# A gated-recurrence and SwiGLU kernel on one core: new dates in its planner, another count of its clock fillers, and another way to narrow its weights

## The chip, the cores and the metric

The kernel runs on one core of one Trainium2 chip. The metric is the device time of one execution in microseconds (us). A core has TensorE (PE, with its weight loads as PEld), VectorE (DVE), ScalarE (ACT), GpSimd (POOL) and SyncE (SP), which here only issues DMAs; ACT and POOL issue some too. Each engine runs its own list of instructions in order and waits for semaphores of the others.

## What is computed

Four sequences of 768 steps with 8 heads of 48 features go through a recurrence with a complex gate per feature. Its output, 3072 tokens of 384 features, goes through a root-mean-square norm and a SwiGLU feed-forward:

```python
mag = np.sqrt(a_re * a_re + a_im * a_im)
scale = np.minimum(mag, 0.999) / (mag + 1e-06)
a_re_n, a_im_n = (a_re * scale, a_im * scale)
for t in range(S):
    new_re = ar * S_re - ai * S_im          # ar, ai: the gate at step t
    new_im = ar * S_im + ai * S_re
    S_re, S_im = (new_re + kv, new_im)      # kv: outer product of k and v at t
    y[:, :, t] = np.einsum('bhd,bhde->bhe', q[:, :, t], S_re)
...
xn = x / rms * rms_g                        # x: y as 3072 x 384
g = xn @ w_gate
silu = g * (1.0 / (1.0 + np.exp(-g)))
val = xn @ w_val
return (silu * val @ w_out)
```

The three weights (384 x 1536, 384 x 1536, 1536 x 384) come as 64-bit floats, all else as 32-bit floats.

## The kernel before

**Tiling.** The 3072 tokens are 24 chunks of 128 steps, six to a sequence. Gates are worked out in *units*: chunk 0, chunk 1, and then two chunks at a time (`gates`, line 1138). A unit loads the gate's parts and q and k, takes the gate's size (stage "size"), running products and a root ("root"), the running angle with sine and cosine ("turn"), and rotates q and k ("rot"): the products go to the tiles `rot` or `kin`. Six DMAs per chunk on SP then bring them from there into the tile `kq`, one partition set at a time (line 1229). `attend` (line 1247) multiplies k by q of a chunk on PE (`bank<-kq`), masks the scores into `am` on VectorE, makes the output y and the new state, and norms it into `xT`. Two chunks are a group of the feed-forward. The first two groups run plainly (`feed`), the other ten with products of sums of blocks, in which fewer block products are needed (`joint`, `forms`).

**Weights.** `narrow` (line 1035) turns a 64-bit float into a 32-bit one in 12 pieces: six of 1536 values per partition (gate and value weights by turns) and six of 768 (output weights). POOL fetches the raw words piece by piece (`fetch`, line 1012), two ahead at most; the fifth fetch also waits for `cleared[1]`, a one-column copy `seen<-kq` on POOL that shows that the second chunk's rotated rows have landed. With `lo` and `hi` the two 32-bit words of a value, ScalarE scales `lo` down to the last three bits, and VectorE shifts `hi` left by three, clears two exponent bits and keeps the sign with one scalar_tensor_tensor (`stt`), and adds `lo`. The integer sum shows in the profile as CUSTOM_DVE_ANT_0.

**The order of the work** is not written by hand. The code first hands each operation to a planner, `Flow`, with a duration, what it reads and writes, and sometimes a due date. `dates` (line 595) derives due dates backwards from the feed-forward's clock and adds a shift per stage from `flow.shift` (line 1675). `schedule` (line 617) plays the operations through a model of the engines and the DMA queue: of those that are ready on an engine it takes the one due first, and the result is each engine's fixed order. A DMA is landed, in this model, a time `load` of service plus `slow` plus 1.0 us after its turn. Neither `slow` nor `load` nor any duration is an instruction; they only move the order. `issue` (line 741) emits everything, so that nearly all rows of the profile bear line 746.

**Fillers.** After idle time PE runs matmuls slowly at first (15 filler records start between 26 and 29 us, 29 between 31 and 34). Where PE has a gap ahead of its next operation before 62 us (`WARM`), the planner puts matmuls without use into it (lines 707 to 713), of rows of `rot`, which show as `bank<-rot`. They can only start once the first rotated rows of the first chunk are written (`started`). The count is made from the gap in the model:

```python
since = max([free["PE"]] + [x["end"] + 0.06 for x in self.warm["after"] if not recent])
step = 0.26 if recent else 0.43
n = int((t - since - 0.25) / step)
```

`recent` holds the last PE operations of any kind, `free["PE"]` is the end of PE's last one, `t` the start of the next.

**Closing check.** At the end of its work the kernel also looks at all raw weights again (`look`, line 1056) and at ranges of the gates; a slower general version runs where a limit is passed, which the inputs here don't.

Of the kernel before, what the change touches and what calls it, by code (L numbers as in the profile page):

```python
# [8 lines left out]
FP32 = mybir.dt.float32  # L9
I32 = mybir.dt.int32  # L10
U32 = mybir.dt.uint32
I16 = mybir.dt.int16
BF16 = mybir.dt.bfloat16
AF = mybir.ActivationFunctionType
ALU = mybir.AluOpType
PSUM = bass.MemoryType.PSUM
# [2 lines left out]
P = 128  # L19
# [481 lines left out]
class Flow:  # L501
# [10 lines left out]
    turn = 0.0  # L512
# [104 lines left out]
    def schedule(self):  # L617
# [3 lines left out]
        free = {}  # L621
# [10 lines left out]
        recent = []  # L632
# [13 lines left out]
        while True:  # L646
# [58 lines left out]
                dur += self.between(o, last)  # L705
                mode, last = o["mode"], o
            if eng == "PE" and self.warm and not claimed and t < self.warm["until"] and all("end" in x for x in self.warm["after"]):
                since = max([free["PE"]] + [x["end"] + 0.06 for x in self.warm["after"] if not recent])
                step = 0.26 if recent else 0.43
                n = int((t - since - 0.25) / step)  # L710
                if n > 0:
                    self.fillers.append((order - 0.5, n))
                    recent.append((since, since + step * n))
            claimed = claimed or o["claims"]
            if eng == "PE":
                busy = sum(min(e, t) - max(b, t - 4.0) for b, e in recent if e > t - 4.0)
# [32 lines left out]
def fast(tc, ctx, qT, kT, v, a_re, a_im, w_gate, w_val, w_out, rms_g, out, H, bad):  # L749

    nc = tc.nc
# [28 lines left out]
    def room(name, shape, dtype=FP32):  # L780
        t = mem.tile(shape, dtype, name=name, tag=name)
        row = 1
        for x in shape[1:]:
            row *= x
        rooms[t.tensor.name] = (name, row * mybir.dt.size(dtype))
        keep.append(t)
        return t
# [122 lines left out]
    width = room("width", [P, 1])  # L910
    warm = room("warm", [P, 1])
    gcol = room("gcol", [P, ND])
    zeros = room("zeros", [P, 2 * C])
    ends = room("ends", [P, ND, N])
    range_ = room("range_", [P, NU])
# [66 lines left out]
    for r in range(ND):  # L982
        o = pick[:, r].rearrange("p (x j) -> p x j", j=2 * ND)[:, :, r::ND]
        copy(o, band.unsqueeze(2).to_broadcast([P, P // H, 2]), late=LATE)
    dma(gcol, rms_g.rearrange("(c p) -> p c", p=P))

# [23 lines left out]
    def fetch(i, piece, raw, eng):  # L1012
        to, ap, c, f = piece
        rows, n = to.shape[1:]
        src = ap.bitcast(I32).rearrange("(c p) f -> p c f", p=P)[:, c, 2 * f:2 * (f + n)]
        raw3 = raw.rearrange("p (c f) -> p c f", c=rows)
        if eng == "POOL" and i >= AHEAD:
            wait = [landed[i - AHEAD]]
        elif eng == "POOL":
            wait = [begun[0]]  # L1020
        else:
            wait = []
        if eng == "POOL" and i in CLEAR:
            wait = wait + [cleared[CLEAR[i]]]
        pace = dict(load=1.9 + 1.0e-3 * raw.shape[1], lead=1.2) if eng == "POOL" else dict(slow=2.5)
        sent = dma(raw3, src, eng, after=wait, **pace)
        if eng == "POOL":
            landed[i] = add("POOL", [(nc.gpsimd.tensor_copy, (), dict(out=junk, in_=raw[0:1, 1:2]))], 0.4,
                            after=[sent])
        words = raw.rearrange("p (n two) -> p n two", two=2)  # L1030
        return words[:, :, 0], words[:, :, 1]

    HALVED = ()

    def narrow(i):
        flow.stage = "w", i
        to, ap, c, f = pieces[i]
        rows, n = to.shape[1:]
        if ap.dtype == FP32:
            dma(to, ap.rearrange("(c p) f -> p c f", p=P)[:, c, f:f + n], "POOL")  # L1040
            return
        flow.stage = "raw", i
        lo, hi = (x.rearrange("p (c f) -> p c f", f=n) for x in fetch(i, pieces[i], places[i], "POOL"))
        flow.stage = "w", i
        t = to.bitcast(I32)
        act(lo, lo.bitcast(U32), AF.Copy, scale=2.0 ** -29)
        step = n // 2 if i in HALVED else n
        for f in range(0, n, step):
            to_, lo_, hi_ = (x[:, :, f:f + step] for x in (t, lo, hi))
            add("DVE", [(nc.vector.tensor_scalar, (),  # L1050
                         dict(out=to_, in0=hi_, scalar1=3, scalar2=None, op0=ALU.logical_shift_left))],
                0.15 + 0.52e-3 * rows * step, [hi_], [to_])
            stt(to_, hi_, 0x3FFFFFFF, to_, ALU.bitwise_or, ALU.bitwise_and)
            tt(to_, to_, lo_, ALU.add)

    def look(i):
        flow.stage = "look", i
# [80 lines left out]
    def gates(u):  # L1138
# [85 lines left out]
        for i, n_ in enumerate(ns):  # L1224
            if i and n_ >= SOLO:
                yield "moves"
            kq = kqs[n_ % 2 if n_ < SOLO else 0]
            flow.stage = "rot", u
            moved[n_] = [dma(kq[r:D2:2 * ND], x, "SP", slow=0.3) for r, x in enumerate(rows[n_])]
            if n_ < 2:  # L1230
                cleared[n_] = copy(seen, kqs[n_ % 2][0:D2, 0, 0:1], eng="POOL")
                cleared[n_]["dur"] = 0.25
            if not i:
                send_decays(u)
# [12 lines left out]
    def attend(n):  # L1247
# [74 lines left out]
        act(sq, yT, AF.Square)  # L1322
        if unit_of[n] in LIGHT:
            for j in range(ND):
                act(yg[:, j], yT[:, j], AF.Copy, scale=gcol[:, j:j + 1])
        else:
            tt(sq[:, 0], sq[:, 0], sq[:, 1], ALU.add)
            tt(sq[:, 0], sq[:, 0], sq[:, 2], ALU.add)
# [52 lines left out]
    def feed(g, xT):  # L1381
# [41 lines left out]
        for i in range(2):  # L1423
            o = bank()[:, 0:DM]
            for f0 in range(0, NF, 4):
                clock[0] += 4 * mm_time(DM) * SPREAD
                mms([(o, h[:, i, f], wo[:, f], f == 0, f == NF - 1) for f in range(f0, f0 + 4)],
                    4 * mm_time(DM), due=clock[0])
            act(ots[i], o, AF.Copy)
        finish(ns)  # L1430

    def finish(ns):
# [186 lines left out]
    for n in range(N):  # L1619
        for x in rest:  # L1620
            pass
        while gated < NU and UNITS[gated][0] <= n:
            rest = gates(gated)
            for x in rest:
                if x:
                    break
            gated += 1
        xT = attend(n)
        g = group_of[n]
        if n == GROUPS[g][-1] and g < WIDE:  # L1630
            if g < PLAIN:
                feed(g, xT)
            else:
                joint(g, sets, range(5))
            if g == FIRST - 1:
                flow.stage = "feed", FIRST
                weight_sums()
                flow.stage = "scale", 0
                for f in range(DF // W):
                    for w_ in (wg, wv):  # L1640
                        for d in range(ND):
                            act(w_[:, f, d], w_[:, f, d], AF.Copy, scale=gcol[:, d:d + 1])
            if g == PLAIN - 1:
                sets = forms()

# [11 lines left out]
    for in_, limit, op in ((ef, P_MIN, ALU.is_ge), (ef, 1.0, ALU.is_le), (range_, 0.0, ALU.is_le),  # L1657
# [15 lines left out]
    flow.warm = dict(after=started, until=WARM, call=[  # L1673
        (nc.tensor.matmul, (banks[3][:, 0:C],), dict(lhsT=filler[:, 0:C], rhs=filler[:, C:2 * C], start=True, stop=True))])
    flow.shift = {
        ("attend", 6): -2.0, ("attend", 10): 27.7, ("attend", 13): -59.0, ("attend", 15): -9.6,
        ("attend", 16): 3.2, ("attend", 18): -0.6, ("attend", 19): 3.8, ("attend", 20): -8.6,
        ("attend", 21): 8.9, ("decay", 2): 9.4, ("feed", 0): 12.3, ("feed", 1): 8.8, ("feed", 2): 0.1,
        ("feed", 3): 33.4, ("feed", 4): 12.1, ("feed", 5): 22.8, ("feed", 6): 10.8, ("feed", 7): 19.1,
        ("feed", 8): -3.7, ("feed", 9): -0.3, ("feed", 11): -8.6, ("form", 3): 18.9, ("form", 5): -0.3,  # L1680
        ("form", 11): -0.7, ("head", 1): 0.4, ("head", 2): -5.2, ("kq", 3): -1.8, ("load", 0): 0.2,
        ("load", 1): -0.9, ("look", 3): 1.0, ("look", 4): -3.5, ("look", 6): 2.0, ("look", 11): 17.2,
        ("look", 13): 50.4, ("look", 17): 28.6, ("norm", 2): -0.7, ("norm", 8): 9.0, ("norm", 9): -8.6,
        ("norm", 12): 1.9, ("norm", 22): -30.7, ("norm", 23): -5.1, ("raw", 0): -5.9, ("raw", 1): 2.7,
        ("root", 2): 4.2, ("root", 5): 0.1, ("root", 9): 0.2, ("root", 10): 0.2, ("root", 11): 0.1,
        ("root", 12): 0.2, ("rot", 1): 91.2, ("rot", 6): 43.0, ("rot", 8): -1.0, ("size", 0): 0.5,
        ("size", 1): -2.6, ("size", 3): 59.1, ("size", 8): 0.9, ("size", 9): -4.8, ("size", 10): 32.3,
        ("size", 11): 3.3, ("size", 12): 29.3, ("state", 1): -32.4, ("state", 3): -12.7, ("state", 6): -11.7,
        ("state", 7): 1.5, ("state", 14): -0.6, ("state", 18): -9.4, ("state", 19): -9.8, ("state", 20): -11.4,
        ("state", 21): -1.1, ("state", 22): 0.4, ("turn", 3): -0.4, ("turn", 5): -0.1, ("turn", 6): 66.3,  # L1690
        ("turn", 7): 41.7, ("turn", 8): 1.9, ("w", 1): 25.0, ("w", 2): -1.5, ("w", 3): -4.7, ("w", 4): 18.1,
        ("w", 5): 37.1, ("w", 10): 9.8, ("y", 3): 0.9, ("y", 6): -2.3, ("y", 12): 17.5, ("y", 14): 3.9,
        ("y", 18): 2.4, ("y", 23): -6.5,
    }
    flow.schedule()
    with tc.manual_schedule():
# [56 lines left out]
```

## Time and profile before

| what | us |
|---|---|
| median of 3 runs | 691.67 |
| lowest to highest run | 690.75 to 694.41 |
| the profiled execution | 691.83 |
| its span in the profile | 690.1 |
| granted TensorE clock, mean | 0.996 |

A row of a timeline has start and length in us, engine, line, operation, output and inputs with shapes, how many it merges, and in brackets the idle time before it with what ended it. A row of the groups has busy us and mean ns behind the first bar, idle time and its releasers behind the second. A row of the stretches has its length, then busy time and number of instructions by engine, the granted clock, the share of the DMA engines and GB/s. A matmul of 32-bit floats shows as two records.

### The profile page before, as it was taken

Reading aid. Unit: us, or ns where it says so; the run is one execution under the profiler, and the core shown is the slowest. Engines: PE = TensorE matmul, PEld = TensorE weight load, DVE = VectorE, ACT = ScalarE, POOL = GpSimd, SP = SyncE. Lnnn points to the kernel's source line nnn. Section 1 sums busy time; section 2 is a strip of 40 time slices with the busy share of each in tenths; the row PEclk is TensorE's granted clock in tenths of the full one; section 3 lists DMA queues with packets and bytes.
Section 4 is the critical chain, followed back from the end, with each engine's and each line's share of the span. In section 5 each row is a group of like instructions: output and inputs, shape, how many; then the busy total and the mean of one; then the engine's idle time right before and its main releaser. Section 6 shows DMA issues by size and latency. Waiting matters only on the chain.

```text
span 690.1 us, 19118 instructions
## 1 busy us (share of the span) xinstructions
PE 652.9 (95%) x7965; PEld 609.6 (88%) x7965; DVE 556.2 (81%) x1026; ACT 499.6 (72%) x864; POOL 63.7 (9%) x109
## 2 busy tenths in 40 slices
PE   0699999999999999999999999989999998999997
PEld 0688887786899999999999999989999998999997
DVE  8969999989998969879989869779879777346563
ACT  8629667895685774874788776867679675799872
POOL 3113031011000100011010100101000000000000
PEclk9999999999999999999999999999999999999999
DMA  9786574355325521354552622556151445735510
GB/s 282 257 230 195 146 208 140 98 128 107 102 54 97 140 34 54 92 117 79 141 89 61 146 53 45 115 107 143 39 107 34 95 128 116 258 95 184 161 47 26
DMA packets 104156, 81.98 MB, mean 119 GB/s; under 512 B 41953, under 2 KB 94561, under 8 KB 104065
## 3 DMA queue, kind: packets, MB, share of 16 engines
q1 hardware_dynamic: 98560, 64.68, 35.0%
q0 software_dynamic: 4416, 15.35, 10.5%
q8 instruction: 63, 1.03, 0.6%
q10 hardware_dynamic: 1088, 0.69, 0.3%
q14 instruction: 29, 0.23, 0.1%
HBM read 55.84 MB, written 4.72 MB: 88 GB/s over the span
## 4 chain that ended last, share of the span: by engine, by line
PE 76%; DVE 8%; issue 4%; SPq 4%; DMA 4%; ACT 3%; POOL 0%; DVEq 0%; POOLq 0%; ACTq 0%
PE bank L746 76%; SPq L746 4%; DVE turns L746 1%; DVE hT L746 1%; DVE t L746 1%; DMA decay<-ends 1%; ACT in L746 1%; ACT t L746 1%; DMA in<-in_w_val_dram 1%; DMA ve<-in_v_dram 1%; DVE rot L746 1%; DVE am L746 1%; ACT L746 1%; DMA vn<-in_v_dram 1%; ACT bank L746 1%
## 5 line engine op out<-in xcount | busy, mean ns | idle before, releaser
L746 PE MATMUL bank<-wo,hT 128*128 128x192 f32 (+1 forms) x696 | 140.7, 350 | 0.0
L746 PEld LDWEIGHTS bank<-wo,hT 128*128 128x128 f32 x696 | 115.0, 190 | 11.6 <-DVE hT L746 0.5
L746 PE MATMUL bank<-xT,wg 128*128 128x128 f32 (+1 forms) x488 | 85.3, 308 | 0.0
L746 PE MATMUL bank<-xT,wv 128*128 128x128 f32 (+1 forms) x488 | 83.2, 303 | 0.0
L746 ACT ACT_TABLE_LOAD x57 | 73.1, 1283 | 9.4 <-DVE rot L746 5.1
L746 ACT ACTIVATE hT<-bank 128x512 f32<-128x512 f32 x100 | 58.4, 596 | 25.0 <-PE bank L746 22.5
L746 PEld LDWEIGHTS bank<-xT,wg 128*128 128x128 f32 x488 | 71.4, 193 | 5.3 <-issue 0.6
L746 PEld LDWEIGHTS bank<-xT,wv 128*128 128x128 f32 x488 | 70.6, 193 | 3.2 <-issue 0.2
L746 POOL TENSOR_TENSOR rs<-ssv,mhalf 128x1 f32<-128x1 f32 x24 | 21.4, 890 | 461.5 <-ACT ssv L746 407.9
L746 DVE COPY_PREDICATED am<-causal,bank 128x512 f32<-128x512 int32 x48 | 34.7, 731 | 22.9 <-PE bank L746 22.8
L746 DVE TENSOR_TENSOR hT<-hT 128x768 f32<-128x768 f32 (+1 forms) x60 | 51.5, 860 | 0.4
L746 PE MATMUL bank<-yg,wg 128*128 128x128 f32 x320 | 50.7, 281 | 0.0
L746 PE MATMUL bank<-yg,wv 128*128 128x128 f32 x320 | 48.8, 275 | 0.0
L746 ACT ACTIVATE bank<-bank 128x512 f32<-128x512 f32 x60 | 35.2, 586 | 17.9 <-PE bank L746 11.4
L746 ACT ACTIVATE sg<-bank 128x256 f32<-128x256 f32 (+1 forms) x72 | 38.5, 536 | 9.2 <-DVE bank L746 4.7
L746 DVE TENSOR_TENSOR hT<-bank,hT 128x512 f32<-128x512 f32 x50 | 34.3, 687 | 13.4 <-ACT bank L746 5.3
L746 PE MATMUL bank<-sums,hT 128*128 128x192 f32 x240 | 44.7, 329 | 0.0
L746 PEld LDWEIGHTS bank<-yg,wg 128*128 128x128 f32 x320 | 42.2, 191 | 1.3 <-issue 0.2
L746 PEld LDWEIGHTS bank<-yg,wv 128*128 128x128 f32 x320 | 42.2, 192 | 0.0
L746 PEld LDWEIGHTS bank<-kq 96*32 96x32 f32 x1536 | 30.5, 110 | 11.2 <-issue 5.1
L746 PEld LDWEIGHTS bank<-sums,hT 128*128 128x128 f32 x240 | 39.1, 190 | 0.4 <-DVE mid L746 0.2
L746 PE MATMUL bank<-kq 96*32 96x128 f32 (+3 forms) x1536 | 36.4, 237 | 3.1 <-DMA decay<-ends 1.9
(217 smaller groups left out, 1451.5 us busy)
## 6 DMA issues: line engine op xcount, KB each, us to landing
kq<-rot SPq DMA_DIRECT2D x84, 128.0 KB, 2.5
kq<-kin SPq DMA_DIRECT2D x60, 128.0 KB, 2.6
kin<-in_q_dram SPq DMA_DIRECT2D x24, 192.0 KB, 2.9
kin<-in_k_dram SPq DMA_DIRECT2D x24, 192.0 KB, 3.3
in<-in_a_re_dram SPq DMA_DIRECT2D x11, 384.0 KB, 4.2
in<-in_a_im_dram SPq DMA_DIRECT2D x11, 384.0 KB, 4.2
out_dram<-ot SPq DMA_DIRECT2D x22, 192.0 KB, 3.0
vn<-in_v_dram SPq DMA_DIRECT2D x20, 192.0 KB, 3.2
```

The source lines that it names most:

```text
L746: fn(*args, **kw)
```

## The change

It has four parts.

1. *Fillers.* The end of what the fillers read now always counts, and the number depends on whether PE was busy for 2 of the last 4 us before the gap; the first nine of a cold gap are taken as slow.

```diff
-                since = max([free["PE"]] + [x["end"] + 0.06 for x in self.warm["after"] if not recent])
-                step = 0.26 if recent else 0.43
-                n = int((t - since - 0.25) / step)
+                since = max([free["PE"]] + [x["end"] + 0.06 for x in self.warm["after"]])
+                left_ = t - since - 0.25
+                hot = sum(e - max(b, since - 4.0) for b, e in recent if e > since - 4.0)
+                n = int(left_ / 0.24 if hot >= 2.0 else left_ / 0.43 if left_ < 3.9 else 9 + (left_ - 3.9) / 0.24)
                 if n > 0:
                     self.fillers.append((order - 0.5, n))
-                    recent.append((since, since + step * n))
+                    recent.append((since, t - 0.25))
```

2. *Narrowing.* ScalarE writes the last bits as a 16-bit number into the lower half of the word `lo` and the sign of `hi` as a 16-bit float (+1 or -1) into its upper half. Adding that word to the shifted `hi` gives sign, exponent and last bits at once, and half the weight's value. The `stt` is gone.

```diff
-        act(lo, lo.bitcast(U32), AF.Copy, scale=2.0 ** -29)
-        step = n // 2 if i in HALVED else n
-        for f in range(0, n, step):
-            to_, lo_, hi_ = (x[:, :, f:f + step] for x in (t, lo, hi))
-            add("DVE", [(nc.vector.tensor_scalar, (),
-                         dict(out=to_, in0=hi_, scalar1=3, scalar2=None, op0=ALU.logical_shift_left))],
-                0.15 + 0.52e-3 * rows * step, [hi_], [to_])
-            stt(to_, hi_, 0x3FFFFFFF, to_, ALU.bitwise_or, ALU.bitwise_and)
-            tt(to_, to_, lo_, ALU.add)
+        low, high = (places[i].bitcast(d).rearrange("p (c f four) -> p c f four", f=n, four=4)[:, :, :, k]
+                     for d, k in ((U16, 0), (BF16, 1)))
+        act(low, lo.bitcast(U32), AF.Copy, scale=2.0 ** -29)
+        act(high, hi.bitcast(FP32), AF.Sign)
+        add("DVE", [(nc.vector.tensor_scalar, (),
+                     dict(out=t, in0=hi, scalar1=3, scalar2=None, op0=ALU.logical_shift_left))],
+            0.15 + 0.52e-3 * rows * n, [hi], [t])
+        tt(t, t, lo, ALU.add)
```

3. *Scales.* The halved weights are made up for by factors of 2: two new columns `gate_col` and `val_col` take the place of `gcol` where weights and the first norms are scaled, and a plain group's output copy gets a scale.

```diff
+    MORE = [1.0 if x.dtype == FP32 else 2.0 for x in (w_gate, w_val, w_out)]
+    act(gate_col, gcol, AF.Copy, scale=MORE[0])
+    act(val_col, gcol, AF.Copy, scale=MORE[1] * MORE[2])
...
-                act(yg[:, j], yT[:, j], AF.Copy, scale=gcol[:, j:j + 1])
+                act(yg[:, j], yT[:, j], AF.Copy, scale=gate_col[:, j:j + 1])
...
-            act(ots[i], o, AF.Copy)
+            act(ots[i], o, AF.Copy, scale=MORE[2])
```

4. *The planner's numbers.* The rotated rows are taken as 1.5 us slower to land from the third chunk on (0.3 before), the first four weight fetches as quicker, and the table of shifts is replaced: 87 entries of -59.0 to 91.2 go, 11 small ones come.

```diff
-        pace = dict(load=1.9 + 1.0e-3 * raw.shape[1], lead=1.2) if eng == "POOL" else dict(slow=2.5)
+        pace = dict(load=1.9 + (0.8e-3 if i < 4 else 1.0e-3) * raw.shape[1], lead=1.2) if eng == "POOL" else dict(slow=2.5)
...
-            moved[n_] = [dma(kq[r:D2:2 * ND], x, "SP", slow=0.3) for r, x in enumerate(rows[n_])]
+            moved[n_] = [dma(kq[r:D2:2 * ND], x, "SP", slow=0.3 if n_ < 2 else 1.5) for r, x in enumerate(rows[n_])]
...
+        ("feed", 1): 5.5, ("feed", 2): 0.1, ("feed", 10): -0.1, ("look", 6): 0.1, ("look", 7): -1.6,
+        ("norm", 22): -0.3, ("root", 3): 0.1, ("rot", 0): 0.5, ("turn", 3): -0.1, ("y", 7): -0.3, ("y", 16): 0.1,
```

More of the change, by code (lines that the diff above doesn't have):

```diff
@@ L13 @@
 BF16 = mybir.dt.bfloat16
+U16 = mybir.dt.uint16
 AF = mybir.ActivationFunctionType
@@ L912, in fast @@
     gcol = room("gcol", [P, ND])
+    gate_col = room("gate_col", [P, ND])
+    val_col = room("val_col", [P, ND])
     zeros = room("zeros", [P, 2 * C])
@@ L1031, in fetch @@
         return words[:, :, 0], words[:, :, 1]
-    HALVED = ()
     def narrow(i):
@@ L1639, in fast @@
                 for f in range(DF // W):
-                    for w_ in (wg, wv):
+                    for w_, col in ((wg, gate_col), (wv, val_col)):
                         for d in range(ND):
-                            act(w_[:, f, d], w_[:, f, d], AF.Copy, scale=gcol[:, d:d + 1])
+                            act(w_[:, f, d], w_[:, f, d], AF.Copy, scale=col[:, d:d + 1])
             if g == PLAIN - 1:
@@ L1675, in fast @@
     flow.shift = {
[L1676 to L1693, printed above, removed]
+        ("feed", 1): 5.5, ("feed", 2): 0.1, ("feed", 10): -0.1, ("look", 6): 0.1, ("look", 7): -1.6,
+        ("norm", 22): -0.3, ("root", 3): 0.1, ("rot", 0): 0.5, ("turn", 3): -0.1, ("y", 7): -0.3, ("y", 16): 0.1,
     }
```

## The prediction

> **What bounds the kernel now.** I read the page's busy shares first.
>
> ```profile
> PE 652.9 (95%) x7965; PEld 609.6 (88%) x7965; DVE 556.2 (81%) x1026; ACT 499.6 (72%) x864; POOL 63.7 (9%) x109
> ```
>
> PE is the bound. Busy time by stage says where it isn't full:
>
> ```profile
> 56.00:120.00 64.00, 62.92 (x651) 53.16 (x651) 61.85 (x87) 48.12 (x68) 12.95 (x16) 1.00 0.57 171
> 120.00:480.00 360.00, 356.24 (x4612) 329.74 (x4611) 313.92 (x594) 263.71 (x441) 29.05 (x44) 1.00 0.43 95
> 480.00:690.00 210.00, 203.61 (x2216) 198.28 (x2215) 136.12 (x275) 153.89 (x297) 6.70 (x12) 0.99 0.39 108
> ```
>
> The columns are PE, PEld, DVE, ACT, POOL. From 56 us on PE is busy 622.8 of 634 us (62.92 + 356.24 + 203.61). So what starts the feed-forward earlier reaches the end nearly one for one. Nearly all idle time of PE lies before 56, and what it is busy with there is not all work. The timeline of PE, then of its neighbours:
>
> ```profile
> 16.95 2.38 PE L746 MATMUL bank<-ot,ot 128*96 128x8 f32 x12 [16.95 <-DVE ot L746]
> 25.70 14.31 PE L746 MATMUL bank<-rot 128*128 128x128 f32 x108 [6.37 <-DVE rot L746]
> 39.94 1.33 PE L746 MATMUL bank<-kq 96*32 96x128 f32 x64
> 45.14 1.33 PE L746 MATMUL bank<-kq 96*32 96x128 f32 x64
> 56.17 2.84 PE L746 MATMUL bank<-xT,wg 128*128 128x128 f32 x24
> ...
> 25.67 3.82 SPq L746 DMA_DIRECT2D kq<-rot  x6
> 31.61 0.49 POOL L746 COPY seen<-kq 96x1 f32<-96x1 f32 x1 [2.92 <-DMA kq<-rot]
> 31.97 1.82 DVE L746 TENSOR_TENSOR rot<-kin,turns 128x768 f32<-128x768 f32 x2
> 32.95 4.78 SPq L746 DMA_DIRECT2D kq<-rot  x6
> 40.80 1.37 DVE L746 COPY_PREDICATED am<-causal,bank 128x512 f32<-128x512 int32 x2 [6.14 <-PE bank L746]
> 41.79 0.89 ACT L746 ACTIVATE kt<-bank 128x384 f32<-128x384 f32 x2 [11.78 <-PE bank L746]
> 47.33 0.80 POOL L746 DMA_DIRECT2D wo<-in_w_gate_dram  x1
> ```
>
> `bank<-rot` is the filler that keeps the clock up: 108 records, two to a matmul, so 54 fillers in 14.31 us. The first chunk's attend (kq, 39.94) stands behind them, though its data had landed by 31.61: **8.3 us of late start made by the fillers themselves**. Others pay too: VectorE is held 6.14 us and ScalarE 11.78 us by that attend, and the fifth weight fetch (47.33), which comes on POOL behind the second `seen`, waits as well.
>
> **The change part by part.**
>
> *Fillers.* Line 708 takes the data's end into account only while no PE work is recent. The decay products (16.95 to 19.33) made it recent, so fillers were counted from about 19.3, while they can start only with rot, 25.70. 54 x 0.26 + 0.25 = 14.3 us from 19.3 puts the planner's start of the attend at about 33.6 at the latest; the real data say 31.6. The new count starts from rot's end: 25.7 + 0.25 to 31.6 or 33.6 leaves 5.65 to 7.65 us, and 9 + (left - 3.9) / 0.24 gives 16 to 24 fillers. What they take, by the records and busy time of the fillers in two stretches:
>
> ```profile
> 26.00:29.00 3.00, 3.00 (x15) 1.00 0.53 149
> 31.00:34.00 3.00, 3.00 (x29) 1.00 0.40 64
> ```
>
> Fifteen filler records in 3 us early, 29 later: 0.40 us and 0.21 us a filler. Nine slow ones and 7 to 15 quick ones take 5.1 to 6.8 us and end at 30.8 to 32.5. With the data at 31.6, the first attend starts at 31.7 to 32.6; I take 32.2, **7.7 us earlier**.
>
> Next is the second chunk. Its six kq transfers are issued from 32.95, over 4.78 us; the first chunk's, issued over 3.82, took from 25.67 to 31.61 from first issue to landing, so the second's are there at 38.9 to 39.9. Its attend therefore can't slide from 45.14 by all of 7.7: in the old order it gains 5.2 to 6.2, middle 5.7, and more if rot of chunk two goes ahead (it ran at 31.97, and its transfers waited in SP's order behind five ve loads). From there to the feed's start the old dates took 56.17 - 45.14 = 11.0 us, with two of the 1.75 us operations of the next part between; I let a little over half of one come through, 1.0: **feed 6.7 us earlier**, with 4.5 (as if the second attend lost 1.2 more) and 9 (7.7 and most of both operations) as bounds. Late next could be the weights of the feed's last third; their fetch (47.33) waits for the second chunk's landing, so it moves up to about 40, as far as the feed does.
>
> *Conversion of the weights.* Per piece a scalar_tensor_tensor on VectorE goes, and a Sign on ScalarE comes:
>
> ```profile
> L746 DVE SCALAR_TENSOR_TENSOR wo<-hT,wo 128x768 int32<-128x768 int32 x4 | 3.8, 954 | 0.0
> L746 DVE SCALAR_TENSOR_TENSOR wv<-wo,wv 128x1536 int32<-128x1536 int32 x2 | 3.5, 1754 | 0.0
> L746 DVE SCALAR_TENSOR_TENSOR wg<-wo,wg 128x1536 int32<-128x1536 int32 x2 | 3.5, 1752 | 0.0
> L746 DVE SCALAR_TENSOR_TENSOR wo<-wo 128x768 int32<-128x768 int32 x2 | 1.9, 952 | 0.0
> L746 DVE SCALAR_TENSOR_TENSOR wv<-hT,wv 128x1536 int32<-128x1536 int32 x1 | 1.8, 1752 | 0.0
> L746 DVE SCALAR_TENSOR_TENSOR wg<-hT,wg 128x1536 int32<-128x1536 int32 x1 | 1.7, 1748 | 0.0
> ...
> L746 ACT ACTIVATE t<-t 128x768 f32<-128x768 f32 x33 | 27.7, 841 | 11.0 <-DVE t L746 10.8
> L746 ACT ACTIVATE wo<-wo 128x1536 int32<-128x1536 uint32 x4 | 6.5, 1633 | 0.0
> ...
> 10.00:120.00 110.00, 93.06 (x1140) 81.62 (x1141) 99.25 (x141) 74.66 (x114) 23.22 (x28) 1.00 0.69 209
> ```
>
> VectorE loses 3.8 + 3.5 + 3.5 + 1.9 + 1.8 + 1.7 = 16.2 us, all within 10 to 120 us, where it is busier than PE (99.25 of 110). The trace has no Sign. By the nearest rows, a 1536-wide one lies between twice 0.84 less one fixed part (about 1.5) and 1.63; a half-size one is about 0.85. I take 1.5: 6 x 1.5 + 6 x 0.85 = 14.1 us on ScalarE, which has 110 - 74.7 = 35.3 us idle there; 7.7 of those go with the fillers, 13.5 remain. That idle hides the Signs; without it up to 14.1 us would show. For the path to the feed's start I count nothing beyond the 1.0 above. Past it, two waits on VectorE may go, 0.62 and 0.46 us; I take **1.0 us**.
>
> *The two new columns.* gate_col and val_col are two tiny ScalarE instructions that wait for gcol:
>
> ```profile
> 8.97 0.59 SPq L746 DMA_DIRECT2D gcol<-in_rms_g_dram  x1
> gcol<-in_rms_g_dram SPq DMA_DIRECT2D x1, 1.5 KB, 10.2
> 85.15 0.55 PE L746 MATMUL bank<-ident,kq 96*128 96x96 f32 x4 [0.62 <-DVE am L746]
> 96.47 0.71 PE L746 MATMUL bank<-ident,kq 96*128 96x96 f32 x6 [0.46 <-DVE xT L746]
> ```
>
> Issued at 8.97, gcol lands near 19.2. Behind a waiting column stand the gates of both first chunks on ScalarE: placed at 17 it would cost them 2 us, placed in the 11.78 us of idle time ahead of 41.79 nothing. The planner picks by due date, and the first reader is the first norm, later than those gates; I take 0. The other scale changes alter a number in an instruction that is there already.
>
> *New dates.* No instruction appears; orders on every engine change. The larger slow for kq from the third chunk on only makes the planner expect what the late transfers show here:
>
> ```profile
> 550.07 0.39 SPq L746 DMA_DIRECT2D in<-in_w_gate_dram  x1
> 562.57 0.39 SPq L746 DMA_DIRECT2D in<-in_w_val_dram  x1
> 572.22 0.99 PE L746 MATMUL bank<-kq 96*32 96x128 f32 x32 [1.93 <-DMA decay<-ends]
> 573.14 1.22 PE L746 MATMUL bank<-xT,wg 128*128 128x128 f32 x4
> 575.86 0.69 PE L746 MATMUL bank<-xT,wv 128*128 128x128 f32 x4
> 464.24 0.52 PE L746 MATMUL bank<-ident,kq 96*128 96x96 f32 x4 [2.14 <-issue]
> ```
>
> SP stood 12 us between two loads of the closing check, the transfers behind the second went out late, and PE waited 1.93 us; then its groups of four matmuls took 1.22 instead of 0.69 until 575.9, some 1.4 us more over three of them. With the 2.14 at 464.24, about 5.5 us after 400 could go. The bounds are those 5.5 gained, and as much lost to new waits of the same kind; I take **2.0 us** gained, nearer to nothing.
>
> **The sum.** 6.7 + 1.0 + 2.0 = 9.7. The profiled execution took 691.83 us (span 690.1), the median is 691.67: 691.83 - 9.7 = 682.1, on the median 682.0.
>
> **The rivals.**
>
> *All of it lands* (0.18): the second attend moves up by the whole 7.7 or more (rot of chunk two goes ahead), VectorE's relief pulls the feed 9 us earlier, and most of the 5.5 go: 691.7 - 9 - 1 - 5 = about 677 down to 673. For it: VectorE's 6.14 us of idle time and 16.2 us of work go in the same stretch. Against: SP's issue, 12 transfers of about 0.6 us and five loads in one queue.
>
> *The head start is spent again* (0.12): the feed starts 4.5 earlier, and the new order makes about 2 to 4 us of waits more than the old one had: 688 to 691. For it: the old order has only about 11 us of PE idle after 56, so there is more to lose than to win. Against: the wait at 572 is on transfers that were expected too early, which the new times correct.
>
> *Slower: Sign isn't in the active table* (0.08). The chip loads an activation table where a function is missing:
>
> ```profile
> L746 ACT ACT_TABLE_LOAD x57 | 73.1, 1283 | 9.4 <-DVE rot L746 5.1 <-issue 2.3 <-DVE kin L746 1.1
> 20.44 1.28 ACT L746 ACT_TABLE_LOAD   x1
> 22.67 1.68 ACT L746 ACTIVATE wo<-wo 128x1536 int32<-128x1536 uint32 x1
> ```
>
> If each of 12 Signs needs its own and the next function loads again, 24 x 1.283 = 30.8 us come to 14.1, 44.9 us on ScalarE where 35.3 - 7.7 = 27.6 are idle. The 17.3 us over delay the rotations and so the attends: 682 + 17.3 = 699, slower than before. It decides from one load per Sign (15.4 + 14.1 = 29.5, just full) upwards. Against it: Copy runs at 22.67 right behind a load for Sin, with none of its own.
>
> The Trainium skill, "ScalarE: Activation LUTs", section "Table sets: the hidden batching unit", says that cheap functions such as relu, copy, identity and abs stand in every set, but Sign is not among those it names there. The Copy row agrees with it; by its wording Sign would be free if it counts as cheap, and the rival's 30.8 us would hold if not. No run here shows a Sign yet.
>
> **How the numbers follow.** Forecast 682.0, chance 0.62, own range 677 to 687. The range 673 to 690 takes in the full landing and most of the spent start, and leaves out the table rival and the tails. About 0.5% is what a measurement of this kernel tells from no change: faster means below 688.2. From forecast 0.62, full landing 0.18 and a third of the spent start 0.04: faster 0.84; same 0.08; slower 0.08.
>
> **What would show it.** Fillers: about 32 to 48 `bank<-rot` records in the first gap and the first kq matmul near 32 us; wrong if it starts after 34, or if VectorE's idle before the first `am` stays above 3 us. Second attend at 38 to 40.5; feed at 47 to 52 instead of 56.17. Conversion: no scalar_tensor_tensor of int32 pieces, 12 new activations at 0.85 and 1.5 us, still 57 table loads or nearly; over 65 would prove the table rival. Dates: PE busy share from the feed's start on at 98% or more; a share below means new waits, and then the time comes out above 687. The forecast is wrong if the feed starts early and PE then starves for the third and fourth chunk or for weights.

## The result and the profile after

| what | us |
|---|---|
| before, median of 4 runs | 691.36 (690.75 to 694.41) |
| after, median of 4 runs | 711.51 (710.88 to 711.96) |
| ratio | 1.0284, 95% interval 1.0256 to 1.0311 |
| predicted | 682.0 (673 to 690) |

The changed kernel is slower by 2.8%. The page's busy shares, which stand in the order of those before:

```profile
PE 659.9 (93%) x7934; PEld 613.3 (86%) x7935; DVE 543.7 (77%) x1014; ACT 551.5 (78%) x883; POOL 72.2 (10%) x109
```

VectorE is busy 12.5 us less (the prediction counted 16.2); ScalarE is busy 51.9 us more, over three times the 14.1 that the prediction gave it. Busy time by stretches says where (length, then PE, PEld, DVE, ACT, POOL, the granted clock, DMA share, GB/s):

```profile
16.00:40.00 24.00, 12.32 (x142) 11.60 (x146) 15.73 (x23) 23.97 (x16) 4.09 (x6) 0.98 0.78 244
40.00:56.00 16.00, 8.53 (x101) 7.64 (x94) 4.94 (x5) 15.13 (x17) 3.61 (x5) 0.50 0.93 228
56.00:120.00 64.00, 55.28 (x563) 47.15 (x565) 44.50 (x64) 63.69 (x60) 7.06 (x14) 0.93 0.50 152
120.00:480.00 360.00, 357.25 (x4456) 328.16 (x4450) 305.57 (x565) 267.16 (x443) 35.10 (x41) 1.00 0.40 87
480.00:710.00 230.00, 225.44 (x2686) 217.74 (x2684) 158.96 (x321) 168.32 (x326) 16.54 (x18) 1.00 0.44 116
```

The kernel before, in the two stretches of these that the prediction doesn't show:

```profile
16.00:40.00 24.00, 16.57 (x124) 16.26 (x128) 17.45 (x27) 12.59 (x16) 4.04 (x6) 1.00 0.74 241
40.00:56.00 16.00, 13.57 (x372) 12.21 (x372) 13.97 (x14) 8.30 (x18) 5.17 (x6) 1.00 0.96 252
```

ScalarE is now busy 102.8 of the 104 us from 16 to 120 (69.0 before). VectorE has 4.94 us of work in 40 to 56, PE 8.53, and PE's mean granted clock is 0.50 there (13.97, 13.57 and 1.00 before): with little to do PE also does that little slowly. From 120 us on PE is as full as before. The loss is made by then, and it stays. PE's timeline (start, length; in brackets the idle time ahead and what ended it) shows who kept it waiting:

```profile
24.26 7.98 PE L748 MATMUL bank<-rot 128*128 128x128 f32 x50 [4.74 <-DVE rot L748]
32.17 1.33 PE L748 MATMUL bank<-kq 96*32 96x128 f32 x64
38.78 0.76 PE L748 MATMUL bank<-ident,kq 96*128 96x96 f32 x4 [4.55 <-DVE am L748]
48.48 1.83 PE L748 MATMUL bank<-vn,kt 128*32 128x48 f32 x48 [7.08 <-ACT kt L748]
51.87 4.69 PE L748 MATMUL bank<-rot 128*128 128x128 f32 x22
56.49 1.33 PE L748 MATMUL bank<-kq 96*32 96x128 f32 x64
65.41 2.84 PE L748 MATMUL bank<-xT,wg 128*128 128x128 f32 x24
91.37 5.49 PE L748 MATMUL bank<-xT,wg 128*128 128x256 f32 x12 [4.07 <-ACT sg L748]
116.67 0.55 PE L748 MATMUL bank<-ident,kq 96*128 96x96 f32 x4 [3.96 <-DVE am L748]
```

The first attend starts at 32.17, where 32.2 was forecast. From there on the path leaves the forecast: the second attend is at 56.49 (45.14 before), the feed at 65.41 (56.17). ScalarE's timeline has the reason for the 7.08 us on `kt`:

```profile
34.19 13.92 ACT L748 ACTIVATE hT<-hT 128x1536 uint16<-128x1536 uint32 x4
47.83 0.59 ACT L748 ACTIVATE kt<-bank 128x384 f32<-128x384 f32 x1
```

Four conversion instructions (the row merges two Copies and two Signs) hold ScalarE for 13.92 us, and the copy of `kt`, which PE waits for, stands behind them. The groups of ScalarE by shape give all 24 instructions of the conversion and the table loads (busy us, mean ns):

```profile
L748 ACT ACT_TABLE_LOAD x62 | 79.5, 1283 | 8.8 <-DVE kin L748 5.5 <-issue 2.3
L748 ACT ACTIVATE wo<-wo 128x1536 bf16<-128x1536 f32 x4 | 14.7, 3676 | 0.0
L748 ACT ACTIVATE wo<-wo 128x1536 uint16<-128x1536 uint32 x4 | 14.5, 3636 | 0.0
L748 ACT ACTIVATE hT<-hT 128x768 uint16<-128x768 uint32 x4 | 7.7, 1936 | 0.0
L748 ACT ACTIVATE hT<-hT 128x768 bf16<-128x768 f32 x4 | 7.7, 1915 | 0.1
L748 ACT ACTIVATE hT<-hT 128x1536 uint16<-128x1536 uint32 x2 | 7.1, 3694 | 0.0
L748 ACT ACTIVATE hT<-hT 128x1536 bf16<-128x1536 f32 x2 | 7.1, 3670 | 0.0
L748 ACT ACTIVATE wo<-wo 128x768 bf16<-128x768 f32 x2 | 3.9, 1926 | 0.0
L748 ACT ACTIVATE wo<-wo 128x768 uint16<-128x768 uint32 x2 | 3.8, 1910 | 0.0
```

`bf16` rows are the Signs, 33.4 us in all; `uint16` rows are the Copies, 33.1 us. Before, the Copies wrote 32 bits, the full-size ones at 1633 ns where they now take 3636. A further element costs (3676 - 1926) / 768 = 2.28 ns.

### The profile page after: what moved, and what is told of

It is laid out like the page before. It is cut to its first block, busy times and chain, and to the rows that moved or that the text cites. A ratio compares the mean times of both kernels' runs of the same rounds, so it can differ in the third digit from the quotient of the medians.

```text
span 710.0 us, 19055 instructions
## 1 busy us (share of the span) xinstructions
PE 659.9 (93%) x7934; PEld 613.3 (86%) x7935; DVE 543.7 (77%) x1014; ACT 551.5 (78%) x883; POOL 72.2 (10%) x109
## 4 chain that ended last, share of the span: by engine, by line
PE 60%; ACT 15%; issue 15%; DVE 4%; DMA 3%; POOL 2%; POOLq 0%; DVEq 0%
PE bank L748 60%; ACT wo L748 4%; ACT hT L748 4%; DMA sq<-rs 2%; ACT L748 2%; ACT turns L748 2%; POOL rs L748 1%; DMA row<-sq 1%; ACT t L748 1%; ACT in L748 1%; DVE turns L748 1%; DVE t L748 1%; DVE kin L748 1%; ACT sg L748 0%; DVE hT L748 0%
## 5 line engine op out<-in xcount | busy, mean ns | idle before, releaser
L748 PE MATMUL bank<-xT,wg 128*128 128x128 f32 (+1 forms) x488 | 87.5, 313 | 6.0 <-ACT sg L748 4.5
L748 POOL TENSOR_TENSOR rs<-ssv,mhalf 128x1 f32<-128x1 f32 x24 | 34.6, 1441 | 483.2 <-ACT ssv L748 398.2
L748 DVE TENSOR_TENSOR hT<-bank,hT 128x512 f32<-128x512 f32 x50 | 34.3, 687 | 14.1 <-PE bank L748 7.9
L748 PE MATMUL bank<-am,ve 128*32 128x128 f32 x768 | 38.8, 286 | 0.1
L748 ACT ACTIVATE t<-t 128x768 f32<-128x768 f32 (+1 forms) x39 | 30.7, 793 | 9.2 <-DVE t L748 9.0
```

The costliest lines, as they stand in the source:

```text
L748: fn(*args, **kw)
```

## The experiments

In kernels named "pinned" every engine keeps the order of the kernel it is made from, and only the emitted instructions differ; the others are planned anew. Save in the first, that is done by replacing the `["calls"]` of an operation, the instructions that it emits, while the planner still sees the operation as it was. All but the probe of the writes are timed against the kernel before on their chip (medians 691.72, 691.32 and 690.55 us). Each expectation sets the theory that ScalarE's conversion is the cause against its rivals.

**Fillers alone** (pinned to the order before):

```diff
     flow.schedule()
+    flow.fillers = [(at, min(n, 25)) for at, n in flow.fillers]
```

> The kernel before, every engine's order kept, with 25 fillers instead of 54 in the first gap and nothing else. Theory A (the prediction's first term holds, and what made the changed kernel slower lies in the weights' conversion on ScalarE): first attend near 32.2 us instead of 39.94, feed 5 to 7 us earlier, 684 to 687 us. Rival B (the head is bound by something else, and the fillers only fill time that is lost anyway): 690 to 692. Rival C (fewer fillers leave the clock low): slower than 693.

684.6 us (683.3 to 695.7), ratio 0.9886 [0.9819, 0.9952]: theory A's time. PE's timeline, from an execution of 687.59 us:

```profile
26.34 7.34 PE L746 MATMUL bank<-rot 128*128 128x128 f32 x50 [6.36 <-DVE rot L746]
33.61 1.34 PE L746 MATMUL bank<-kq 96*32 96x128 f32 x64
39.96 1.33 PE L746 MATMUL bank<-kq 96*32 96x128 f32 x64 [0.34 <-DMA kq<-rot]
46.38 0.30 PE L746 MATMUL bank<-am,ve 128*32 128x128 f32 x2 [2.19 <-issue]
54.04 2.84 PE L746 MATMUL bank<-xT,wg 128*128 128x128 f32 x24
```

The second attend is 5.2 us earlier and waits for its transfers, as the prediction's 5.2 to 6.2 had it. The first attend comes at 33.61, not near 32.2, and the feed is only 2.1 us earlier, not 5 to 7: behind a stall of 2.19 us whose cause the profile doesn't show, PE's granted clock is 0.79 from 40 to 56 us (1.00 before). By the first matmul of the joint part 0.6 us are left of the head start (172.78 against 173.36). The kernel gains 7.1 us by the medians (3 to 13 by the interval), and 4.2 us of span in its profile; 3.6 of these lie behind that point. So the gain at the end isn't shown to be the feed's head start.

**New order with the old conversion** (pinned to the order after; the scales are 1 again):

```diff
-        act(low, lo.bitcast(U32), AF.Copy, scale=2.0 ** -29)
-        act(high, hi.bitcast(FP32), AF.Sign)
+        last = act(low, lo.bitcast(U32), AF.Copy, scale=2.0 ** -29)
+        sign = act(high, hi.bitcast(FP32), AF.Sign)
...
-        tt(t, t, lo, ALU.add)
+        plus_ = tt(t, t, lo, ALU.add)
+        sign["calls"] = []
+        last["calls"] = [(nc.scalar.activation, (), dict(out=lo, in_=lo.bitcast(U32), func=AF.Copy, scale=2.0 ** -29))]
+        plus_["calls"] = [(nc.vector.scalar_tensor_tensor, (), dict(out=t, in0=hi, scalar=0x3FFFFFFF, in1=t, op0=ALU.bitwise_or,
+                                                                   op1=ALU.bitwise_and))] + plus_["calls"]
```

> The changed kernel, every engine's order kept, with the old conversion of the weights in its place: one 32-bit Copy on ScalarE, the scalar_tensor_tensor back on VectorE, scales of 1. Theory A (the two 16-bit outputs on ScalarE, 66.5 us against 15.3 us, are the loss): 682 to 692 us. Rival D (the new dates are a worse order in themselves): 700 us or more.

694.12 us, ratio 1.003 [1.0003, 1.0057]: 2 us above theory A's range and far below rival D's. Without the new conversion 17.4 of the 20.2 us lost are gone, yet no gain is left. This order was planned without the `stt`; against the kernel with 32-bit outputs in the last pair of experiments, putting the `stt` back and taking the Sign out costs 7 to 8 us here (7 by the ratios to the kernel before, 8 by the medians).

**Old order with the new conversion** (pinned to the order before, 54 fillers; the factors of 2 are left out, so the output's scale is another):

```diff
-        act(lo, lo.bitcast(U32), AF.Copy, scale=2.0 ** -29)
...
+        last = act(lo, lo.bitcast(U32), AF.Copy, scale=2.0 ** -29)
+        last["calls"] = [(nc.scalar.activation, (), dict(out=low, in_=lo.bitcast(U32), func=AF.Copy, scale=2.0 ** -29)),
+                         (nc.scalar.activation, (), dict(out=high, in_=hi.bitcast(FP32), func=AF.Sign))]
...
-            stt(to_, hi_, 0x3FFFFFFF, to_, ALU.bitwise_or, ALU.bitwise_and)
+            stt(to_, hi_, 0x3FFFFFFF, to_, ALU.bitwise_or, ALU.bitwise_and)["calls"] = []
```

> The kernel before, every engine's order kept, 54 fillers, with the new conversion alone: two 16-bit outputs on ScalarE in place of the Copy, no scalar_tensor_tensor. The factor of 2 is not made up for, so the output is of another size. Theory A: ScalarE gets about 51 us more before 120 us, of which it has 35 idle: 705 to 725 us. Rival D (the dates are the loss): 688 to 695.

723.08 us, ratio 1.0437 [1.0359, 1.0516]. So the conversion alone loses 31.4 us, more than the whole change, in an order in which nothing else is new. It is an order that was not planned for it.

**What the writes cost by themselves.** Ahead of the kernel before, 24 activations on one scratch tile, each form at its own width so that its row can be told. The core of it, with `two` the view of every second word and `by(x, d, s, k)` that of every s-th element of type d:

```diff
+    X, Y = hT[:, 0:1536], hT[:, 1536:3072]
+        for n, o, i, f in ((768, two(X), two(X), AF.Copy),
+                           (764, by(X, BF16, 4, 1), two(X), AF.Copy),
+                           (760, flat16(Y, BF16), X, AF.Copy),
+                           (756, by(Y, BF16, 2, 1), X, AF.Copy),
...
+                           (748, two(X), two(X), AF.Sign),
+                           (744, by(Y, BF16, 4, 1), two(X), AF.Copy),
+                           (740, two(Y), X, AF.Copy),
+                           (736, by(X, U16, 4, 0), two(X).bitcast(U32), AF.Copy),
...
+                           (724, by(Y, BF16, 4, 1), two(X), AF.Sign)):
+            act(o[:, 0:n], i[:, 0:n], f, due=-300.0)
```

> The kernel before with 24 ScalarE instructions ahead of its work that differ in output type and step, twice each, told apart by their width (724 to 768). Theory E (a 16-bit output to every eighth byte is what is slow): about 1.9 us for the widths 764, 744, 736 and 724, and 0.8 to 0.9 us for 16 bits side by side (760, 752) and for all 32-bit outputs, Sign among them (748). Rival F (any 16-bit output is slow): 760, 752 and 756 also 1.9 us. Rival G (Sign itself, or writing into the words that are being read): 748 slow, or 744 quick.

ScalarE's groups by shape (a single execution, 735.74 us):

```profile
L747 ACT ACTIVATE hT<-hT 128x764 bf16<-128x764 f32 x2 | 3.8, 1886 | 0.0
L747 ACT ACTIVATE hT<-hT 128x744 bf16<-128x744 f32 x2 | 3.7, 1847 | 0.1
L747 ACT ACTIVATE hT<-hT 128x736 uint16<-128x736 uint32 x2 | 3.7, 1828 | 0.1
L747 ACT ACTIVATE hT<-hT 128x724 bf16<-128x724 f32 x2 | 3.6, 1803 | 0.1
L747 ACT ACTIVATE hT<-hT 128x756 bf16<-128x756 f32 x2 | 2.1, 1040 | 0.1
L747 ACT ACTIVATE hT<-hT 128x768 f32<-128x768 f32 x2 | 1.8, 876 | 0.5 <-DVE hT L747 0.5
L747 ACT ACTIVATE hT<-hT 128x748 f32<-128x748 f32 x2 | 1.7, 858 | 0.1
L747 ACT ACTIVATE hT<-hT 128x760 bf16<-128x760 f32 x2 | 1.7, 836 | 0.1
```

All rows that write 16 bits to every eighth byte take 1803 to 1886 ns: Copy or Sign, `bf16` or `uint16`, in place (764, 736) or to another tile (744, 724). Sign that writes 32 bits at the same step takes 858, like Copy at 876. 16 bits side by side take 836 (866 from an input with a step, at a width of 752), to every fourth byte 1040. It is the narrow output together with the step, and not Sign, the kind of 16-bit number or the place. (In all four slow rows the input has a step of eight bytes too, as in the conversion.)

**Old conversion, planned anew** (the changed kernel with the `stt` back, scales of 1 and the old operations' durations in the planner):

```diff
-        act(low, lo.bitcast(U32), AF.Copy, scale=2.0 ** -29)
-        act(high, hi.bitcast(FP32), AF.Sign)
+        act(lo, lo.bitcast(U32), AF.Copy, scale=2.0 ** -29)
...
+            stt(to_, hi_, 0x3FFFFFFF, to_, ALU.bitwise_or, ALU.bitwise_and)
```

> The changed kernel with the old conversion of the weights, planned anew by its planner, which now knows true costs for it: new filler count, new dates and landing times. Theory A (the dates are good once the planner's costs are true; what was lost beyond the 16-bit outputs was an order made for costs that don't exist): 682 to 688 us. Rival D (the new dates give a worse order in themselves): 692 us or more, like the same conversion in the changed kernel's order, 694.

709.21 us, ratio 1.0274 [1.0234, 1.0314]: theory A missed, and not by the conversion's price. The planner puts the second chunk's `xT` late on VectorE (its timeline, then PE's):

```profile
74.62 0.54 DVE L748 TENSOR_TENSOR xT<-yg,bank 128x384 f32<-128x384 f32 x1
```

```profile
75.22 2.93 PE L748 MATMUL bank<-xT,wg 128*128 128x128 f32 x12 [13.23 <-DVE xT L748]
```

That one wait is 13.23 us. The same conversion in the pinned order took 694.12, 15.1 us less. So these dates did not carry over to the old operations' costs; a kernel planned anew tells of its new order as well as of its edit.

**The planner knows the true cost** (the changed kernel, planned anew):

```diff
-        act(low, lo.bitcast(U32), AF.Copy, scale=2.0 ** -29)
-        act(high, hi.bitcast(FP32), AF.Sign)
+        for o in (act(low, lo.bitcast(U32), AF.Copy, scale=2.0 ** -29), act(high, hi.bitcast(FP32), AF.Sign)):
+            o["dur"] = 0.2 + 2.25e-3 * rows * n
```

> The changed kernel whose planner is told what the 16-bit outputs take (0.2 + 0.00225 us an element), so that it orders around them. Theory A (66.5 us of them are more than ScalarE has free before 120 us, whatever the order): 700 to 712 us. Rival H (the loss is that the planner counted on 1.5 us, and an order that knows 3.65 hides it): below 695.

721.26 us, ratio 1.0444 [1.04, 1.0487]: above theory A's range, and against rival H. Knowing the cost didn't help with these dates; ScalarE is busy 63.83 of the 64 us from 56 to 120 again. Whether dates made for this cost would hide it wasn't tried.

**Sign in 32 bits.** ScalarE writes the sign as a 32-bit float into `lo`, and the Copy goes; the last three bits of each weight are left out. Once planned anew (the edit below), once pinned to the order before with 25 fillers, where the same Sign takes the Copy's place, the `stt` emits nothing and the two columns and the scales are those of the change:

```diff
-        act(low, lo.bitcast(U32), AF.Copy, scale=2.0 ** -29)
-        act(high, hi.bitcast(FP32), AF.Sign)
+        act(lo.bitcast(FP32), hi.bitcast(FP32), AF.Sign)
```

> The changed kernel with one 32-bit Sign into the word of the last bits in place of both 16-bit outputs: the last three bits of a weight are left out (a step of 2 to the -20 of its value), and VectorE has no scalar_tensor_tensor. Planned anew with a duration that is true. Theory A: 15 us on ScalarE, 16.2 us less on VectorE, 680 to 688 us. Rival D: 692 or more.

> The kernel before in its own order, 25 fillers in the first gap and the 32-bit Sign in place of Copy and scalar_tensor_tensor, scales as in the change. If VectorE's 16.2 us matter on the way to the feed, 2 to 5 us less than the 684.6 of the 25 fillers alone: 680 to 683. If they are hidden by the second chunk's transfers: 684 to 686.

Planned anew 686.9 us, ratio 0.9948 [0.9921, 0.9974]. Pinned 687.72, ratio 0.9947 [0.9925, 0.9968], above both ranges that were expected and no better than the 684.6 of the fillers alone, though VectorE has 16.2 us less to do: in the old order the relief brought nothing that shows at the end. (In the two profiles the joint part starts 1.0 us earlier with it, at 171.81 against 172.78.) One of the pinned kernel's ten executions took 2309.87 us; why isn't known.

**Width of the outputs alone** (pinned to the order after: the same instructions in the same places, first both outputs in 32 bits, where Sign overwrites the last three bits, then only the Copy's; the first edit is shown):

```diff
-        act(low, lo.bitcast(U32), AF.Copy, scale=2.0 ** -29)
-        act(high, hi.bitcast(FP32), AF.Sign)
+        one, two = act(low, lo.bitcast(U32), AF.Copy, scale=2.0 ** -29), act(high, hi.bitcast(FP32), AF.Sign)
+        one["calls"] = [(nc.scalar.activation, (), dict(out=lo, in_=lo.bitcast(U32), func=AF.Copy, scale=2.0 ** -29))]
+        two["calls"] = [(nc.scalar.activation, (), dict(out=lo.bitcast(FP32), in_=hi.bitcast(FP32), func=AF.Sign))]
```

> The changed kernel, every engine's order and every instruction kept, but with 32-bit outputs of the Copy and the Sign in the conversion, so that they take the 1.6 us that the planner counted on. The Sign overwrites the last three bits of a weight, which are left out. Theory A (the output's size is the whole loss; the order is as good as the planner took it for): 680 to 690 us. Rival D (the new order loses 9.5 us by itself, as the old conversion in it showed): 692 to 697.

> The same order with the Copy in 32 bits and the Sign in 16: half of the 51 us too many on ScalarE stay. Theory A: some 26 us more than planned against about 28 idle, with waits in the first 60 us: 692 to 703, between the run with both outputs in 32 bits and the changed kernel's 711.5. If the two 16-bit outputs don't count by their time, it is at either end.

With both at 32 bits 686.14 us, ratio 0.9929 [0.9894, 0.9965]; with the Sign's alone at 16 bits 696.17, ratio 1.0084 [1.0061, 1.0107]; with both at 16 bits it is the changed kernel, 711.51. Three steps of one dose, in one order, and both new ones in the range that theory A gave them. Groups, stretches and PE's timeline of the kernel with both at 32 bits:

```profile
L748 ACT ACTIVATE wo<-wo 128x1536 f32<-128x1536 f32 x4 | 6.5, 1633 | 0.0
L748 ACT ACTIVATE wo<-wo 128x1536 int32<-128x1536 uint32 x4 | 6.4, 1609 | 1.9 <-DMA wo<-in_w_val_dram 1.9
```

```profile
40.00:56.00 16.00, 15.06 (x218) 13.77 (x217) 8.57 (x10) 12.90 (x17) 4.44 (x9) 0.93 1.13 300
56.00:120.00 64.00, 61.55 (x665) 50.05 (x664) 55.76 (x81) 56.37 (x79) 7.79 (x11) 1.00 0.53 148
```

```profile
31.84 1.33 PE L748 MATMUL bank<-kq 96*32 96x128 f32 x64 [0.58 <-DMA kq<-rot]
38.21 4.33 PE L748 MATMUL bank<-rot 128*128 128x128 f32 x22
42.47 1.33 PE L748 MATMUL bank<-kq 96*32 96x128 f32 x64
52.31 2.84 PE L748 MATMUL bank<-xT,wg 128*128 128x128 f32 x24
```

PE has 15.06 and 61.55 us of work where the changed kernel had 8.53 and 55.28, and the clock 0.93 in place of 0.50. That the loss ends early shows in the first matmul of the joint part, from PE's timelines of the kernel before, the changed one and the one with 32-bit outputs:

```profile
173.36 0.71 PE L746 MATMUL bank<-yg,in 128*128 128x128 f32 x4
```

```profile
199.03 0.71 PE L748 MATMUL bank<-yg,in 128*128 128x128 f32 x4
```

```profile
173.13 0.71 PE L748 MATMUL bank<-yg,in 128*128 128x128 f32 x4
```

199.03 - 173.13 = 25.9 us between the last two, and 711.51 - 686.14 = 25.4 at the end (24.5 by the two ratios). From there to the end the two take the same time, 511.0 and 511.2 us: the whole loss lies ahead of the joint part.

## Why the prediction was wrong

**The step that failed** is the price of the conversion: "I take 1.5: 6 x 1.5 + 6 x 0.85 = 14.1 us on ScalarE". It measured 33.4 us. The bounds were drawn from rows that write 32 bits, and the new instructions write 16 bits at a step of eight bytes, which no row of before showed. The Copies were taken as unchanged, though the diff changes their output in the same way: 33.1 us, 17.8 more than the 6.5 + 3.7 + 3.3 + 1.8 = 15.3 of before. So ScalarE got 51.2 us more, not 14.1, and of the 35.3 idle us that were to hide them 27.6 were left by the prediction's own count. By that count 51.2 - 27.6 = 23.6 us stick out; the change of width alone costs 25.4. That the two are so near is partly luck: with only the Sign at 16 bits ScalarE's 24 instructions take 33.3 + 15.4 = 48.7 us, the same count gives 48.7 - 15.3 - 27.6 = 5.8, and the kernel takes 10.0 us more than at 32 bits (696.17). The count knows nothing of the waits that one long instruction makes, nor of PE's clock. At 32 bits the 24 instructions take 30.4 us (the sum of their groups), close to the 14.1 + 15.3 = 29.4 of the prediction, and the time is 686.14, in the forecast's own range of 677 to 687, though not by the forecast's path (below).

A rule of the Trainium skill would have given the same wrong price: "ScalarE: Activation LUTs", section "What ACT_TABLE_LOAD costs", states 186 ns + 0.833 ns an element for an ACTIVATE with immediate scale and bias, and the same rate for fp32 and bf16. The probe agrees with it for 16 bits side by side (836 ns for 760 elements, where 819 is an estimate by the rule) and not at a step of eight bytes (1886 ns for 764, where the estimate is 822).

**The slower rival** had the right place, a ScalarE too full for 27.6 us of idle time, and the wrong mechanism. Sign brought no table load: the loads went from 57 to 62, but the new order with the old conversion, which has no Sign, shows 62 as well, and the old order with the 12 Signs shows 57. So the five come from the order. In the probe Sign costs 858 ns beside Copy's 876.

**Fillers**: the late start was there, its worth was not. The first attend was forecast for 32.2 and came at 32.17, in part by luck: 25 fillers took 7.98 us where 16 to 24 were to take 5.1 to 6.8, but they could start at 24.26 and not at 25.70. With the fillers alone it came at 33.61. The **6.7 us** at the feed, with bounds of 4.5 and 9, are 2.1 with the fillers alone and 3.9 in the new order with 32-bit outputs (52.31). The prediction counted fillers in the first gap only. The new count also puts 11 of them (22 records, 38.21 to 42.5) ahead of the second attend, where the kernel before had two. That attend stands right behind them at 42.47, not at 38 to 40.5, though its rows had landed by 40.8 (the last of their six transfers was issued at 31.9, and none took over 8.9 us to land). In the changed kernel the same 11 stand from 51.87 to 56.5; what they add to the loss there was not tested.

Nor did the feed's head start reach the end "nearly one for one". At the first joint matmul 0.6 of 2.1 us are left with the fillers alone, and 0.2 of 3.9 in the new order with 32-bit outputs (173.13 against 173.36). On the way PE waited 2.5 us for `xT` in the latter (0.5 before), and 1.3 for `xT` and 1.0 for rows of `kq` with the fillers alone.

**VectorE's relief**, 1.0 us: nothing at the end in the old order (687.72 against 684.6 without it, intervals overlapping), 7 to 8 us in the new one (694.12 against 686.14), which was planned for it.

**The two columns**, 0 us: no wait of PE on them was seen; the two instructions take 0.26 and 0.22 us in the changed kernel, at 34.1 and 49.9.

**New dates**, 2.0 us with bounds of 5.5 either way: in range. The two late waits of before, 2.14 and 1.93 us, are not among those of the changed kernel. From the first joint matmul to the end the kernel before takes 516.7 us and the three others in its order 513.1 to 514.3; the four kernels in the new order (the changed one among them) take 510.7 to 511.2, with no less work on PE there (6317 records against 6286 to 6288). So the new order gains 2 to 6 us there. One profile of each kernel can't tell how much of that spread in the old order is chance.

So the price of one form of instruction explains the 25.4 us. With that price right the kernel gains about 5 us (ratio 0.9929), but of the 5.8 us of span between the profiles of before (690.1) and of 32-bit outputs (684.3), 5.6 lie behind the first joint matmul and 0.2 ahead of it. The forecast's largest term, the early feed, would not have come out as counted even then.

## What to carry to other kernels

Price an instruction by what it reads and writes, type and step of its output included, and when a diff changes an operand of an old instruction, price that one anew too; where no row has the form, a few instructions of that form in front of the kernel settle it in one profile. Where idle time is to hide new work, work out from what price on it no longer does (here 27.6 us, less than twice the estimate) and let the range reach past that point. Count what a new rule does in every gap, and not only in the one that it was made for. And judge an edit in a planned kernel at a fixed order first: planning anew moved the time by 15.1 us with the old conversion (709.21 against 694.12) and by 9.8 with the true price (721.26 against 711.51).

## What the runs showed of the hardware

- ScalarE writes 16-bit outputs at a step of eight bytes at 2.28 ns for each further element. With the fixed part that is 1886 / 764 = 2.5 ns an element in the probe; at a step of four bytes it is 1040 / 756 = 1.4, side by side 836 / 760 = 1.1, and for 32-bit outputs at a step of eight bytes 876 / 768 = 1.1. The Trainium skill, "SBUF — State Buffer", section "Door 1: The DMA port swizzle", states that access is at full rate while two or more hits fall on a 16-byte line. At a step of eight bytes 16 and 32 bits both have two, so that rule doesn't tell 1886 from 876 ns; what does isn't known from these runs.
- PE's mean granted clock was 0.50 over 40 to 56 us in the changed kernel, with waits of 4.55 us that end at 38.78 and 7.08 that end at 48.48. Starving PE was paid twice here, in the idle time and in the matmuls after it: the 48 `vn,kt` records that took 1.83 us there took 0.86 in the kernel before (PE's timeline):

```profile
42.98 0.86 PE L746 MATMUL bank<-vn,kt 128*32 128x48 f32 x48
```
